# RWKV recurrence with a split-precision channel MLP: Q as one scan over padded decays, batch 0's state sum moved from TensorE to VectorE, and a new order table

## The chip, the cores and the metric

The kernel runs on one core of one Trainium2 chip. The metric is the device time in microseconds of one execution, lower is better. The kernel before was run three times: 462.59, 463.63 and 464.78 us, median 463.63. The profiled execution took 464.79 us.

## The reference

Two parts follow each other. The first is a recurrence over 768 time steps for 4 batches x 8 heads of width 48, the second a token mix of rank 32 and a channel MLP with a hidden layer of 1536.

```python
for t in range(S):                                   # B, H, S, D = 4, 8, 768, 48
    cur = einsum('bhd,bhe->bhde', u * k[t], v[t])
    y[t] = einsum('bhd,bhde->bhe', r[t], state + cur)
    state = w[t][..., None] * state + einsum('bhd,bhe->bhde', k[t], v[t])
x = y with heads side by side                         # (4, 768, 384)
xt = x.transpose(0, 2, 1)
u = x + (xt @ U @ V).transpose(0, 2, 1)               # U: 768 x 32, V: 32 x 768
out = u + maximum(u @ w_ch1, 0) @ w_ch2               # 384 -> 1536 -> 384
```

## The kernel before, in words

**Chunks.** The 768 steps of a batch are cut in 6 chunks of 128, so there are 24 chunks, numbered 0 to 23 (batch 0 has 0 to 5). In a chunk the heads lie in NP = 4 pairs j, two heads on the 128 partitions, time along the columns. Decays w are turned into two running products by scans on VectorE: F, from the end of the chunk backwards (`scan_f`, L393, four scans of 128, one for each pair), and Q, the reciprocal of the whole product times the products from the start (`first_q`, L402, a reciprocal of four columns, then `scan_q`, L407, four scans of 127). The scans add the tile `zeros`, a broadcast of one column of the PSUM tile `bank`, which also holds dS, the state increment of a chunk. The steps of a chunk, by the names that the table of the order uses: LW, LRK, LV, LKR load; F, T (totals), R and Q as told; RP and KS scale r by Q and k by F; MD or RK, RU, RED make the diagonal, SEL and SEL2 put it in A; AM (L519) makes the scores in PSUM, CP (L522) copies them into A under a mask; KT and KN turn k; DS (L529) makes dS; ZM multiplies the state by the next chunk's total decay; YA and YZ (L589 to L616) make the output, XE copies it out, XT and XN turn it for the token mix.

**State.** In chunks 1 to 4 of batch 0, ZP (L538) first puts the old state into dS by a matmul with the identity, DS adds to it, and ZM reads the sum from PSUM. In the other batches DS stands alone, ZA (L561, VectorE) adds the old state, and ZM reads SBUF.

**Weights and MLP.** Weights come as 64-bit numbers and are decoded and split in a high and a low part, a piece of 128x384 at a time: AB and E on ScalarE, C1 (L271), C2 (L278), SG, ADD (L295), HI, and SUB (L343) for the low part. w1 has pieces 0 to 11 (named w10 to w111), w2 has pieces w20 to w211. Each half batch then runs 12 up-projections UP b.half.f (L805) and 3 x 4 parts of the down-projection DN b.half.ct.part (L840), each nine matmuls of 384 columns; HH and HL (L818) split a hidden block in high and low. DN 0.0.2.0 needs w28, DN 0.0.2.1 needs w29, and so on. GSL is the last step of a batch's token mix.

**Order.** Nothing is scheduled by the compiler here. `ORDER` (L52 to L93) is a string with three characters for each of the 1438 steps: two for the step's number, one for its engine and for how many filler matmuls `warm` issues on TensorE ahead of it. `plan` turns it into a list; each engine runs its steps in that list's order, and a step that has to wait holds up all that stands behind it on its engine. `caps` gives the buffers of each kind: one for the scores, three for MLP results in PSUM, two for w.

```python
zeros = zero.broadcast_to([P, P])
copy(eng, st["tot"], st["F"][:, :, 0])
ENG[eng].tensor_tensor(out=rk[:, 0], in0=rk[:, 0], in1=st["Q"], op=ALU.mult)
```

Of the kernel before, what the change touches and what calls it, by code (L numbers as in the profile page):

```python
# [38 lines left out]
def channel_order():  # L39
# [18 lines left out]
    "5K00518u04+08d06004-05L01M05p05M18f15w00k15-01v00612909L05i01L08Z09200U06605q00J08g18v06F05j05r05m01N01O11u0"
    "0W08c05y14Y08a06704Z06808b15Q05R06G08h00V08x08y15n08W01P16909K05o16H00X01w01Q00Y05s00Z11x00F05t01y18m08z08+0"
    "0a06I01R18i08j19316A01z06B00G06J09008n06C02R02B06D00b06N06E09N00m01B06K06L01D08q0Ao08w01E01+09406M08k09501C0"  # L60
    "1F18-09U01-09O18l01G19P00o0Af06O06P06S06T06X06W16Q09802A02C09606U09n06Y06b06V08o02D06Z09M08p09906a02E19A0970"
    "9S00n09109C09D06f00p02T00q16x09Q06R12F12G09V01H00r19B09a07102H06g09b06h09W10s01T00t19m06y07208r01V06z01U01W0"
    "1k01m01I07306c07701X11l09R16l02S09X01Y10u09p01n02U01Z01a07806m09v01o01p12V09F09G09u09Y09e00w09r09s09Z02W19c0"
    "0v06d12j07906n0A006e09H01q06u00x01r00y00z19d06r02X06v02l06+06w02I01s02k02-06s12Y10+12006t06-19E10-0A102K02Z0"
    "7409t17006i02m02J02n01017509I02o17602109o07S03102p02a02q02r06o02202L02302402s02519f06j06p07T02M03Z02N1380A20"
    "AC09h02b0260271280DA09i06q07U06k02d0A402O07W07a07X02t02c02u02v02e02w02P02x02f12Q13H02y03002g02h07Y03A07b09w0"
    "2z03203Q03302i13903402+13B07A07B03503I03K03603C03D1AE03J03707c03L07C07D07G07H07V13E0AD03S03F03R09q19j09x17d0"
    "9y13M13T03G13U03a07E07Z07I07J03N17M07K07k0AF07F03O17L07h03c07l03d03P19T0Ae03b09J03e1AK13f17m07N09z03V0AS03W0"
    "9+0AM07i07j03g07e0AN08907f17g03h13X0AG0AL08A08B0AO17t09g17z07u03Y0A507v0AT09-1A307O0Ap0Aq07+07-0800An07n0AH0"
    "8107o0AI0D-0AJ08207P0A70AP0A80A61AQ1Db07Q0AU08Y1ES0AW09k07q0Ah0Aj0Ak0AR0AV0Al07R0Am07p07r1830Ar0A90DZ0Dj0Di0"  # L70
    "Dk07s09l07w0DJ0Au0As0AZ0Aa0Ag0Ab08408s0Da0DK0850DL18t0Dc08C07x07y08608D0870880DM0Ac0E90At08E08F0De0Df0DN1Ad0"
    "Av0AX0Ai0AY0D90DC0Aw0Dd0DE0Ax0E00AA0AB08I08J0DH1EA0EB08K0Dg1DF0DG1Ay0DB0EC0DO1Dl08L0Dm0Az0A-0A+08M0B00Dh0E20"
    "B10DR0E80E70E40E50B20DP0Dn0Do18O0B30Et0FT0DS08P0B40B50B60B70DI0B808Q0E308G0DQ1B90DD08R0FU0Ew0Dp0BA0ER0BD0BE0"
    "DT0BB1BF0FV0DV0BG1Ea0Dr08S08H08N0BC0E61Ds0C70BH0Eu0BW0DU1C80BK0Ey0Eb0Ez0BX1ED0E+1BL0BY0BT0EE0Dq1BM0BI1BJ0BQ0"
# [71 lines left out]
def rwkv_moe_kernel(ctx, tc, wT, rkT, vN, rkN, uB, uT, uD, U, V, w1, w2, out):  # L146
# [35 lines left out]
    zeros = zero.broadcast_to([P, P])  # L182
# [168 lines left out]
    def chunk(g):  # L351
# [8 lines left out]
        def load_w():  # L360
            st["w"] = sb2.tile([P, NP, P], F32, tag="w", name=f"w_{g}", bufs=W_BUFS)
            nc.sync.dma_start(st["w"].rearrange("p j t -> p (j t)"), wT[b, c])

        def load_w2():
            st["w2"] = sb2.tile([P, NP, P], F32, tag="w", name=f"w2_{g}", bufs=W_BUFS)
            nc.sync.dma_start(st["w2"].rearrange("p j t -> p (j t)"), wT[b, c])
# [23 lines left out]
        def scan_f():  # L390
            F = st["F"] = sb2.tile([P, NP, P], F32, tag="F", name=f"F_{g}")
            for j in range(NP):
                nc.vector.tensor_tensor_scan(  # L393
                    out=F[:, j, ::-1], data0=st["w"][:, j, ::-1], data1=zeros, initial=1.0, op0=ALU.mult, op1=ALU.add
                )
# [669 lines left out]
```

## Time and profile before

| what | value |
|---|---|
| median of three runs | 463.63 us (462.59 to 464.78) |
| the profiled execution | 464.79 us |
| its span | 463.1 us, 9864 instructions |
| mean granted TensorE clock | 0.989 of full |
| busy: TensorE, VectorE, ScalarE, GpSimd | 442.9, 308.4, 165.2, 122.7 us |
| first matmul of the MLP (L805) | 68.02 us from the start |
| last matmul (L840) begins | 458.21 us from the start |

The span runs from the first to the last instruction, the run's time has 1.7 us more around it. PE is TensorE, DVE is VectorE, ACT is ScalarE, POOL is GpSimd. Busy time of PE counts a matmul from its issue to its modelled end, and matmuls overlap in the pipeline, so a PE that is 96% busy does not show by itself how much it could still take; the gaps between its instructions and what ended them tell more. Waits name the instruction that came last before an engine went on. The chain of waits is followed back from the last instruction.

### The profile page before, as it was taken

How to read it: one execution, taken by the hardware profiler on the slowest of the kernel's cores; microseconds unless marked ns; L12 is line 12 of the kernel's file. 1: busy time of each engine (PE TensorE's matmuls, PEld its weight loads, DVE VectorE, ACT ScalarE, POOL GpSimd, SP SyncE). 2: the span in 40 equal slices, each digit the busy share in tenths (PEclk: the TensorE clock that was granted, in tenths of full speed). 3: DMA queues.
4: the chain of work that ended last, by engine and by line, in shares of the span. 5: the costliest groups of instructions: out<-in, count | busy, mean ns of one | idle time of the engine just before them, and what ended most of it. 6: DMA issues, size and time to landing. Idle time of an engine off the chain costs nothing.

```text
span 463.1 us, 9864 instructions
## 1 busy us (share of the span) xinstructions
PE 442.9 (96%) x4046; PEld 406.6 (88%) x4049; DVE 308.4 (67%) x653; ACT 165.2 (36%) x406; POOL 122.7 (27%) x127
## 2 busy tenths in 40 slices
PE   8988979899998999999999999999999999999996
PEld 4766558889997989999999989999999899999995
DVE  8898999999865969847685847877166152434410
ACT  4786888796732322123103230411023101300300
POOL 4667667414513346213123220110020010000000
PEclk9799999999998999999999999999999999999999
DMA  7876844374234425114221642201120000110001
GB/s 272 324 253 207 280 146 131 102 272 144 70 93 139 127 84 155 64 48 140 74 89 38 200 141 71 69 33 47 52 64 24 18 17 18 45 42 0 35 18 38
DMA packets 21361, 48.46 MB, mean 105 GB/s; under 512 B 2496, under 2 KB 9024, under 8 KB 21312
## 3 DMA queue, kind: packets, MB, share of 16 engines
q1 hardware_dynamic: 21312, 47.79, 31.3%
q8 instruction: 33, 0.54, 0.5%
q14 instruction: 16, 0.13, 0.1%
HBM read 43.06 MB, written 4.72 MB: 103 GB/s over the span
## 4 chain that ended last, share of the span: by engine, by line
PE 75%; DVE 18%; ACT 3%; issue 2%; DMA 1%; DVEq 0%; ACTq 0%; SPq 0%
PE f L840 29%; PE f L805 28%; PE aps L519 4%; DVE Q L407 3%; PE y L589 2%; DVE F L393 2%; PE bank L529 2%; PE y L599 2%; DVE A L522 1%; DVE hl L818 1%; PE y L612 1%; DVE cva_w L271 1%; DVE cva_w L278 1%; PE trx L649 1%; PE trk L507 1%
## 5 line engine op out<-in xcount | busy, mean ns | idle before, releaser
L805 PE MATMUL f<-u,w1h 128*128 128x384 f32 x576 | 149.9, 341 | 5.6 <-DVE hl L818 5.6
L805 PEld LDWEIGHTS f<-u,w1h 128*128 128x128 f32 x576 | 103.7, 189 | 8.0 <-DVE hl L818 7.3
L840 PE MATMUL f<-hh,w2h 128*128 128x384 f32 x288 | 99.4, 345 | 0.0
L840 PE MATMUL f<-hl,w2h 128*128 128x384 f32 x288 | 97.8, 339 | 0.0
L840 PE MATMUL f<-hh,w2l 128*128 128x384 f32 x288 | 97.3, 338 | 0.4 <-DVE w2l L343 0.4
L805 PE MATMUL f<-u,w1l 128*128 128x384 f32 x288 | 97.5, 338 | 0.0
L818 DVE SCALAR_TENSOR_TENSOR hl<-f,hh 128x384 fp32r<-128x384 f32 x96 | 52.3, 552 | 34.9 <-ACT hh L812 34.0
L812 ACT ACTIVATE hh<-f 128x384 fp32r<-128x384 f32 x55 | 27.0, 496 | 118.1 <-PE f L805 118.1
L840 PEld LDWEIGHTS f<-hh,w2l 128*128 128x128 f32 x288 | 54.0, 188 | 0.7 <-DVE w2l L343 0.7
L805 PEld LDWEIGHTS f<-u,w1l 128*128 128x128 f32 x288 | 54.4, 189 | 0.0
L840 PEld LDWEIGHTS f<-hl,w2h 128*128 128x128 f32 x288 | 54.2, 188 | 0.1
L840 PEld LDWEIGHTS f<-hh,w2h 128*128 128x128 f32 x288 | 54.0, 187 | 0.2 <-issue 0.2
L459 POOL TENSOR_SCALAR_AFFINE_SELECT A<-dv 128x512 f32<-128x512 f32 x32 | 21.5, 679 | 85.0 <-PE y L599 45.9
L393 DVE TENSOR_TENSOR_SCAN F<-w,bank 128x128 f32<-128x128 f32 x96 | 32.3, 398 | 11.2 <-DMA w<-in_wT 6.5
L407 DVE TENSOR_TENSOR_SCAN Q<-w,Q,bank 128x127 f32<-128x127 f32 x96 | 38.0, 458 | 2.6 <-ACT Z L570 1.2
L814 DVE TENSOR_SCALAR hh<-f 128x384 fp32r<-128x384 f32 x41 | 22.4, 550 | 24.6 <-PE f L805 24.6
L855 DVE TENSOR_TENSOR xT<-f,xT 128x384 f32<-128x384 f32 x24 | 13.2, 551 | 35.9 <-PE f L840 35.9
L522 DVE COPY_PREDICATED A<-maskf,aps 128x1024 f32<-128x1024 uint32 x24 | 31.3, 1304 | 5.7 <-PE aps L519 5.7
L519 PEld LDWEIGHTS aps<-rk 48*128 48x128 f32 x384 | 24.5, 195 | 6.1 <-issue 3.0
L519 PE MATMUL aps<-rk 48*128 48x128 f32 x384 | 29.1, 293 | 0.6 <-POOL rk L414 0.6
L414 POOL TENSOR_TENSOR rk<-rk,Q 128x512 f32<-128x512 f32 x14 | 21.8, 1558 | 27.1 <-DVE Q L407 21.5
L764 POOL TENSOR_TENSOR u<-xT,u 128x384 fp32r<-128x384 f32 x9 | 10.5, 1173 | 62.9 <-ACT u L758 62.2
(125 smaller groups left out, 592.9 us busy)
## 6 DMA issues: line engine op xcount, KB each, us to landing
rk<-in_rkT SPq DMA_DIRECT2D x24, 512.0 KB, 4.2
raw_w<-in_w SPq DMA_DIRECT2D x24, 384.0 KB, 5.1
w<-in_wT SPq DMA_DIRECT2D x30, 256.0 KB, 2.8
kr<-in_rkN SPq DMA_DIRECT2D x18, 384.0 KB, 3.4
v<-in_vN SPq DMA_DIRECT2D x24, 224.0 KB, 3.4
out_dram<-xT SPq DMA_DIRECT2D x24, 192.0 KB, 1.9
raw_V<-in_V SPq DMA_DIRECT2D x1, 192.0 KB, 4.1
raw_U<-in_U SPq DMA_DIRECT2D x1, 192.0 KB, 5.7
```

What stands on the lines that cost most here:

```text
L393: nc.vector.tensor_tensor_scan(out=F[:, j, ::-1], data0=st["w"][:, j, ::-1], data1=zeros, initial=1.0, op0=ALU.mult, op1=ALU.add)
L407: nc.vector.tensor_tensor_scan(out=Q[:, j, 1:P], data0=st["w"][:, j, 0 : P - 1], data1=zeros[:, 1:P], initial=Q[:, j, 0:1], op0=ALU.mult, ...
L414: ENG[eng].tensor_tensor(out=rk[:, 0], in0=rk[:, 0], in1=st["Q"], op=ALU.mult)
L459: nc.gpsimd.affine_select(out=A[:, i], in_=dv[:, NP * i : NP * i + NP].unsqueeze(2).broadcast_to([P, NP, P]), pattern=[[0, NP], [1, P]], c ...
L519: nc.tensor.matmul(aps[:, i, j, :], rk[r, 1, j, :], rk[r, 0, j, :], start=True, stop=True)
L522: nc.vector.copy_predicated(flat(st["A"]), mask8, flat(st["aps"]))
L805: nc.tensor.matmul(ps, wt[:, f, ct, :], u[ct][:, z], start=(n == 0), stop=(n == 8))
L812: nc.scalar.activation(hh, d["ps", f], AF.Relu)
L814: nc.vector.tensor_scalar(out=hh, in0=d["ps", f], scalar1=0.0, scalar2=None, op0=ALU.max)
L818: nc.vector.scalar_tensor_tensor(out=hl, in0=d["ps", f], scalar=0.0, in1=hh.bitcast(F32), op0=ALU.max, op1=ALU.subtract)
L840: nc.tensor.matmul(d["o", ct], wt[:, 4 * ct + part, f - 3 * part, :], hid[f][z], start=(part == 0 and n == 0), stop=(part == 3 and n == 8),)
L855: nc.vector.tensor_tensor(out=o, in0=d["o", ct], in1=o, op=ALU.add)
```

## The change

The decays are stored in segments of SEG = 129 columns, of which column 0 is padding with the value 1. `first_q` writes the four reciprocals into this padding of the w tile, and `scan_q` is one scan of 4 x 129 = 516 columns from the initial value 1: at the end of a segment the running product is back at 1, and the next padding multiplies by that pair's reciprocal. The Q tile has the same segments; RP reads their first 128 columns. F, the check of w (`check_w`) and the loads are changed to the new layout, a load of w being 129/128 of what it was. Q's tile is taken by step Q, no longer by step R, and R now uses w. In batch 0, ZP and the accumulation on top of it are gone: DS writes dS alone, and ZA and ZM work as in the other batches, with four ZA more on VectorE.

```diff
+SEG = P + 1
-    zeros = zero.broadcast_to([P, P])
+    zeros = zero.broadcast_to([P, NP * SEG])
...
-            st["w"] = sb2.tile([P, NP, P], F32, tag="w", name=f"w_{g}", bufs=W_BUFS)
+            st["w"] = sb2.tile([P, NP, SEG], F32, tag="w", name=f"w_{g}", bufs=W_BUFS)
...
         def first_q():
-            st["Q"] = sb2.tile([P, NP, P], F32, tag="Q", name=f"Q_{g}")
-            nc.vector.reciprocal(st["Q"][:, :, 0], st["F"][:, :, 0])
+            nc.vector.reciprocal(st["w"][:, :, 0], st["F"][:, :, 0])
 
         def scan_q():
-            Q = st["Q"]
-            for j in range(NP):
-                nc.vector.tensor_tensor_scan(
-                    out=Q[:, j, 1:P], data0=st["w"][:, j, 0 : P - 1], data1=zeros[:, 1:P], initial=Q[:, j, 0:1],
-                    op0=ALU.mult, op1=ALU.add,
-                )
+            st["Q"] = sb2.tile([P, NP, SEG], F32, tag="Q", name=f"Q_{g}")
+            flat = lambda t: t.rearrange("p j s -> p (j s)")
+            nc.vector.tensor_tensor_scan(
+                out=flat(st["Q"]), data0=flat(st["w"]), data1=zeros, initial=1.0, op0=ALU.mult, op1=ALU.add
+            )
...
-                        dS[r, j, i * D : i * D + D], kn[:, j, r], v[:, j, r], start=not carry,
-                        stop=not carry or j == NP - 1,
+                        dS[r, j, i * D : i * D + D], kn[:, j, r], v[:, j, r], start=True, stop=True,
...
-            if carry:
-                zp = step("ZP " + nm, "PE", state_old, [old["z"]], take=[buf["dS"]], use=[old["buf"]["Z"]])
-                ds = step("DS " + nm, "PE", state_add, [kn, lv, zp], use=[buf["dS"], buf["kn"], buf["v"]])
-            else:
-                ds = step("DS " + nm, "PE", state_add, [kn, lv], take=[buf["dS"]], use=[buf["kn"], buf["v"]])
-            from_ps = c == 0 or carry
+            ds = step("DS " + nm, "PE", state_add, [kn, lv], take=[buf["dS"]], use=[buf["kn"], buf["v"]])
+            from_ps = c == 0
...
 ORDER = (
-    "3i03j03k03n03p03q03v03s14800703w+4B04903m03o13x03r13y00804a04b03+60900A04D01b01105104000B03-03z14J14G04E04K2"
+    "3i03j03n03v03p03k04803q03o03r03w+4B04903x04D04E03s04003+04a03-04d00703m04b01b01105104A03y03z14100900804J04G0"
...
```

All 40 lines of the table are new. 197 steps that are in both kernels change their engine: HH mostly swaps between ScalarE and VectorE (22 one way, 18 the other), and XN (8 of them), KN, T, XE, XU, RP, KS, SEL, SUB, ADD and others move. In sum VectorE has 11 steps fewer, ScalarE 8 more, GpSimd 7 more, and TensorE the four ZP fewer. The fillers on TensorE go from 49 half units to 64: MD 1 has 7 more ahead of it, DS 0 has 5, AM 1 has 7, DS 2 has 6, and KT 0, VM V1, MD 2 and AM 4 lose 10 together. No copy in the diff gets a choice of engine that it did not have; the three PSUM copies of the change's short description can only be such reassignments by the table.

**The first place: VectorE in chunks 3 to 6.** In a name such as F_5_606 the 5 is the chunk and 606 the buffer's own number; `bank_94` holds dS and the zeros. Before:

```order
L522 COPY_PREDICATED A_3_444<-maskf_102,aps_3_557 128x1024
L393 SCALAR_TENSOR_TENSOR F_5_606<-w_5_545,bank_94 128x128 x4
L402 RECIPROCAL Q_5_611<-F_5_606 128x4
L393 SCALAR_TENSOR_TENSOR F_6_616<-w_6_550,bank_94 128x128 x4
L407 SCALAR_TENSOR_TENSOR Q_5_611<-w_5_545,Q_5_611,bank_94 128x127 x4
L522 COPY_PREDICATED A_4_664<-maskf_102,aps_4_593 128x1024
```

and after the change:

```order
L407 SCALAR_TENSOR_TENSOR Q_4_528<-w_4_295,bank_94 128x516
L394 SCALAR_TENSOR_TENSOR F_5_549<-w_5_423,bank_94 128x128 x4
L272 TENSOR_SCALAR cva_w1_2_547<-cva_w1_2_547 128x384
L549 TENSOR_TENSOR Z_2_570<-bank_94,Z_1_466 128x384
L402 RECIPROCAL w_5_423<-F_5_549 128x4
L325 TENSOR_TENSOR Vst_118<-vm_0_443,Vst_118 32x384
L521 COPY_PREDICATED A_3_531<-maskf_102,aps_3_579 128x1024
```

The four Q scans are one row of 516 columns, the reciprocal goes to w, and a ZA (L549) that reads `bank` stands between the scans.

**The second place: VectorE in chunks 9 to 11**, at the end of batch 0's MLP. Before:

```order
L522 COPY_PREDICATED A_9_1717<-maskf_102,aps_9_1433 128x1024
L818 SCALAR_TENSOR_TENSOR hl_0_1_7_1810<-f1_0_1_7_1774,hh_0_1_7_1809 128x384
L402 RECIPROCAL Q_10_1834<-F_10_1665 128x4
L407 SCALAR_TENSOR_TENSOR Q_10_1834<-w_10_1442,Q_10_1834,bank_94 128x127 x4
L414 TENSOR_TENSOR rk_10_1606<-rk_10_1606,Q_10_1834 128x512
L818 SCALAR_TENSOR_TENSOR hl_0_1_8_1837<-f1_0_1_8_1813,hh_0_1_8_1836 128x384
L447 TENSOR_REDUCE dv_10_1876<-kr_10_1719 128x8
L855 TENSOR_TENSOR xT_0_0_337<-f2_0_0_2_1644,xT_0_0_337 128x384
L393 SCALAR_TENSOR_TENSOR F_11_1936<-w_11_1690,bank_94 128x128 x4
```

and after the change:

```order
L806 SCALAR_TENSOR_TENSOR hl_0_1_7_1815<-f1_0_1_7_1804,hh_0_1_7_1814 128x384
L413 TENSOR_TENSOR rk_10_1319<-rk_10_1319,Q_10_1774 128x512
L394 SCALAR_TENSOR_TENSOR F_11_1836<-w_11_1772,bank_94 128x128 x4
L402 RECIPROCAL w_11_1772<-F_11_1836 128x4
L521 COPY_PREDICATED A_9_1690<-maskf_102,aps_9_1426 128x1024
L802 TENSOR_SCALAR hh_0_1_5_1874<-f1_0_1_5_1856 128x384
```

The copy of the scores CP 9 (A_9) stood eight rows ahead of F 11; now F 11 stands ahead of CP 9.

## Rows read from the trace of the kernel before

**Rows 1.** Page, part 1: busy us, share of the span, instructions.
```profile
PE 442.9 (96%) x4046; PEld 406.6 (88%) x4049; DVE 308.4 (67%) x653; ACT 165.2 (36%) x406; POOL 122.7 (27%) x127
```

**Rows 2.** Busy time in four stretches (us from the start), PE clock, DMA, GB/s.
```profile
0.00:68.00 68.00, 58.55 (x779) 40.67 (x782) 61.02 (x143) 49.23 (x129) 43.18 (x47) 0.95 0.73 245
68.00:114.00 46.00, 42.46 (x380) 39.66 (x376) 45.11 (x88) 37.71 (x77) 22.52 (x21) 1.00 0.50 168
114.00:160.00 46.00, 43.36 (x412) 40.55 (x411) 33.98 (x73) 18.88 (x52) 14.06 (x15) 0.96 0.33 104
160.00:459.00 299.00, 298.55 (x2484) 285.68 (x2482) 168.11 (x351) 59.39 (x152) 42.95 (x46) 1.00 0.20 64
```

**Rows 3.** Waits of PE: total us, times, longest.
```profile
PE f L805 <- DVE hl L818: 5.6, 5, 1.9
...
PE f L840 <- DVE w2l L343: 0.4, 1, 0.4
```

**Rows 4.** Waits of DVE from 0 to 135 us: total, times, longest.
```profile
...
DVE Q L407 <- ACT Z L570: 1.2, 1, 1.2
...
DVE Q L407 <- PE bank L529: 0.8, 1, 0.8
DVE F L393 <- PE bank L529: 0.7, 1, 0.7
DVE F L393 <- PE bank L538: 0.6, 1, 0.6
```

**Rows 5.** DVE groups, 0 to 114 us: count | busy us, mean ns | idle before.
```profile
L407 DVE TENSOR_TENSOR_SCAN Q<-w,Q,bank 128x127 f32<-128x127 f32 x40 | 15.8, 457 | 2.3 <-ACT Z L570 1.2 <-PE bank L529 0.8
L393 DVE TENSOR_TENSOR_SCAN F<-w,bank 128x128 f32<-128x128 f32 x40 | 13.4, 397 | 2.5 <-DMA w<-in_wT 0.9 <-PE bank L529 0.7 <-PE bank L538 0.6
...
L343 DVE TENSOR_TENSOR w1l<-cva_w,w1h 128x384 fp32r<-128x384 f32 x4 | 4.5, 1118 | 0.0
...
L561 DVE TENSOR_TENSOR Z<-bank,Z 128x384 f32<-128x384 f32 x2 | 1.1, 555 | 0.2 <-PE bank L529 0.2
```

**Rows 6.** DVE in order of time from 5 us: start, us, instruction.
```profile
...
5.38 1.59 DVE L407 TENSOR_TENSOR_SCAN Q<-w,Q,bank 128x127 f32<-128x127 f32 x4
6.89 0.66 DVE L418 TENSOR_TENSOR rk<-rk,F 128x508 f32<-128x508 f32 x1
7.47 1.35 DVE L393 TENSOR_TENSOR_SCAN F<-w,bank 128x128 f32<-128x128 f32 x4
8.73 0.66 DVE L271 TENSOR_SCALAR cva_V<-cva_V 128x192 f32<-128x192 f32 x1
```

**Rows 7.** All engines in order of time, from 71 us.
```profile
...
75.22 0.35 DVE L271 TENSOR_SCALAR cva_w<-cva_w 128x384 f32<-128x384 f32 x1
...
78.41 2.13 DVE L271 TENSOR_SCALAR cva_w<-cva_w 128x384 f32<-128x384 f32 x2
...
79.11 1.21 POOL L418 TENSOR_TENSOR rk<-rk,F 128x508 f32<-128x508 f32 x1
```

**Rows 8.** Chain of waits, 136 to 145.5 us: start, us, what.
```profile
...
136.31 0.52 PE bank L529 x16
...
136.85 1.36 DVE F L393 x4
...
142.33 3.00 PE f L805 x9
```

**Rows 9.** Two stretches, columns as in Rows 2.
```profile
12.80:20.00 7.20, 7.20 (x73) 5.73 (x75) 7.02 (x15) 5.05 (x18) 5.08 (x5) 0.53 0.85 311
142.00:146.00 4.00, 3.67 (x15) 3.24 (x17) 1.66 (x4) 1.19 (x3) 1.59 (x2) 0.58 0.64 214
```

**Rows 10.** Chain of waits, around 115 us.
```profile
...
115.00 3.15 PE f L805 x18
118.14 1.59 PE f L840 x9
```

**Rows 11.** Chain of waits, around 22 us.
```profile
...
21.74 0.75 PE bank L538 x2
```

More of the change, by code (lines that the diff above doesn't have):

```diff
@@ L58 @@
[L58 to L62, printed above, removed]
@@ L360, in load_w @@
         def load_w():
[L361 to L362 removed]
+            st["w"] = sb2.tile([P, NP, SEG], F32, tag="w", name=f"w_{g}", bufs=W_BUFS)
+            nc.sync.dma_start(st["w"].rearrange("p j s -> p (j s)"), wT[b, c])
         def load_w2():
[L365 to L366 removed]
+            st["w2"] = sb2.tile([P, NP, SEG], F32, tag="w", name=f"w2_{g}", bufs=W_BUFS)
+            nc.sync.dma_start(st["w2"].rearrange("p j s -> p (j s)"), wT[b, c])
         def load_rk():
@@ L393, in scan_f @@
                 nc.vector.tensor_tensor_scan(
-                    out=F[:, j, ::-1], data0=st["w"][:, j, ::-1], data1=zeros, initial=1.0, op0=ALU.mult, op1=ALU.add
+                    out=F[:, j, ::-1], data0=st["w"][:, j, SEG - 1 : 0 : -1], data1=zeros[:, 0:P], initial=1.0, op0=ALU.mult, op1=ALU.add
                 )
@@ L421, in check_w @@
             nc.scalar.activation(
-                junk, st[which].bitcast(U32), AF.Relu, bias=b_max, scale=2.0**-23, accum_out=guard[:, g : g + 1]
+                junk, st[which][:, :, 1:SEG].bitcast(U32), AF.Relu, bias=b_max, scale=2.0**-23, accum_out=guard[:, g : g + 1]
             )
@@ L426, in chunk @@
         st["tots"] = step("T " + nm, "DVE", totals, [f], use=[buf["F"]], alt="ACT")
-        rc = step("R " + nm, "DVE", first_q, [f], take=[buf["Q"]], use=[buf["F"]])
-        q = step("Q " + nm, "DVE", scan_q, [rc], use=[buf["w"], buf["Q"]])
+        rc = step("R " + nm, "DVE", first_q, [f], use=[buf["F"], buf["w"]])
+        q = step("Q " + nm, "DVE", scan_q, [rc], take=[buf["Q"]], use=[buf["w"]])
         rp = step("RP " + nm, "DVE", scale_r, [q, lr], use=[buf["Q"], buf["rk"]], alt="Pool")
@@ L529, in state_add @@
                     nc.tensor.matmul(
-                        dS[r, j, i * D : i * D + D], kn[:, j, r], v[:, j, r], start=not carry,
-                        stop=not carry or j == NP - 1,
-                    )
-        carry = b == 0 and c > 0
-        def state_old():
-            flat_z = lambda t: t.rearrange("p j n -> p (j n)")
-            nc.tensor.matmul(flat_z(dS), ident, flat_z(old["Z"]), start=True, stop=False)
+                        dS[r, j, i * D : i * D + D], kn[:, j, r], v[:, j, r], start=True, stop=True,
+                    )
         on = c < NCH - 1
@@ L887, in recurrence @@
                 st, vt = (full(xtp, "xT", f"{n}_{j}") for n in ("st", "vt"))
-                nc.sync.dma_start(chunks(wt), wb[:, :, j * P : (j + 1) * P])
+                nc.sync.dma_start(chunks(wt), wb[:, :, j * SEG + 1 : (j + 1) * SEG])
                 nc.sync.dma_start(chunks(rt), rb[:, 0, j])
@@ L1020, in chunked @@
         return t
-    wT = chunked(w, 1.0).reshape(B, NCH, P, NP * P)
+    wT = np.ones((B, NCH, P, NP, SEG), f32)
+    wT[..., 1:] = chunked(w, 1.0)
+    wT = wT.reshape(B, NCH, P, NP * SEG)
     rkT = np.stack([chunked(r, 0.0), chunked(k, 0.0)], axis=3)
```

75 lines of the change are left out of this document (40 added, 35 removed).

## The prediction

> **What bounds the kernel now.** The page's busy shares come first [rows 1]: TensorE 96%, VectorE 67%. They are averages over stages with different limits, so the second view is busy time by stretch [rows 2]. Read its VectorE column (the third): 61.0 of the first 68 us, 45.1 of the next 46, then 34.0 of 46, then 168 of 299. Read its TensorE column (the first): 9.5 us idle in the first 68 us, 3.5 in the next 46, 2.6 up to 160 us, and 0.45, the last drain, in the 299 us after that. So the run has two halves. Up to about 114 us VectorE is full and TensorE takes what it is fed; from 160 us on TensorE is full. The end moves with the moment at which TensorE has caught up with its feeders, and with little else. VectorE work that is saved after 160 us is worth nothing: TensorE covers it, and that cover is 299 us long.
>
> The third view, the waits of TensorE [rows 3], says which feeder ends last: HL on VectorE, 5.6 us in five waits, and once the low part of a w2 piece, 0.4 us. VectorE's own waits [rows 4] are few: four of them, 3.3 us together, are scans that read the zeros in `bank` and stand behind something that reads or writes dS in the same tile.
>
> **The scans.** Four Q scans take 1.51 us (5.38 to 6.89), four F scans 1.26 us (7.47 to 8.73) [rows 6]. Forty of each lie before 114 us [rows 5], so ten chunks. One scan of 516 columns is not in the trace. Upper bound: four F scans, 4 x 128 = 512 columns with four starts, 1.27 us. Lower bound: the F rows without three of their four starts. A scan is recorded with 397 ns and follows the next after 315, so some 80 ns are pipeline; three starts of that size leave 1.02 us. I take 1.15, the middle, so 0.36 us saved for a chunk (0.24 to 0.49), 3.6 us over ten chunks. The reciprocal is as long as before; 1% more to load is hidden by loads that run a chunk ahead.
>
> **The gate.** What counts is VectorE's work ahead of a step that TensorE needs, plus TensorE's work left behind it. I counted steps in both orders up to DN 0.0.2.1, the down-projection part that needs w29 on VectorE; DN steps around here are where TensorE waited for a w2 piece. VectorE: ten Q scans give back 3.6. Four ZA in batch 0 cost 4 x 0.5 = 2.0 (0.55 recorded, some 0.5 back to back [rows 5]). The table moves eight more steps of other kinds ahead of it (two SUB, two ADD, two HI and others) at some 0.5 us, 4.0, and one F fewer, 1.3. The SUB rows go up to 1.1 us [rows 5], so this could be 1 more. Sum: -3.6 + 2.0 + 4.0 - 1.3 = +1.1 us. TensorE: one UP more is done by then, 3.15 / 2 = 1.6 us [rows 10], and one DS fewer, 0.5 us [rows 8], so 1.1 us less is left. **The gate therefore moves by 0.0** (-1.3 to +2.2 from the two prices above): the scans' time is spent on work that the new order pulls ahead. That is the main reason why I expect little.
>
> At intermediate steps VectorE comes earlier: up to GSL 0 the steps of other kinds fall by 3.6 us and four ZA add 2.0, and eight Q scans give 2.9, so some 4.5 us. The MLP would start at about 63.5 us instead of 68. It is given back by the gate above.
>
> **ZP.** Its four matmul pairs (0.75 us each [rows 11], 3.0 in sum) leave TensorE in the first 68 us, where it idles for 9.5 [rows 2]; the new fillers stand there too. I cost both at nothing; VectorE is the cover. [...] Fillers that kept the clock up there would find VectorE in the way.
>
> **Early waits of VectorE.** Two of the four have lost their cause: ScalarE no longer reads `bank` to make Z in chunks 1 to 4 (1.2 us), and there is no ZP to write it (0.6) [rows 4]. In exchange four ZA on VectorE must wait for DS on TensorE, and F, R and Q queue behind them. One such wait of 0.6 us is my guess from the size of the rows that stay (0.7, 0.8). Net **-1.2 us**, bounds -3.3 (all four go) and +1.4 (each ZA waits 0.8, less the 1.8).
>
> **The stop at 140 us.** F 11 began 0.02 us after the matmul on `bank` ended [rows 8], behind it stood Q, CP and HL, and TensorE then waited 1.9 us for HL [rows 3]. From 142 to 146 us the clock was 0.58 [rows 9], which cost 4 x 0.42 = 1.7 us more: 3.6 in all. In the new order F 11 stands ahead of CP 9, and the scores AM 10 need the one score buffer that CP 9 frees; DS 10 comes after AM 10, so F 11 cannot wait for DS 10. That stop is gone as such. But the same stretch now has CP 9 behind F 11, so something else may be late; I take 40% of it, **-1.4 us**, bounds -3.6 and the rival below.
>
> **GpSimd.** Five two-input steps fewer run on GpSimd ahead of the gate, eleven steps more after it. The same C1 takes 0.35 us alone and over 1 us with a GpSimd step in the same microseconds [rows 7]. [...] I keep the plain sum, since no row tells which instructions would meet.
>
> **Sum.** 464.8 for the profiled execution, 0.0 - 1.2 - 1.4 = -2.6, so 462.2. The median of the runs lies 1.2 under the profiled execution, so **461.0 us** for the median. A measurement of this kernel can tell some 0.5%, 2.3 us, from no change; the forecast lies just beyond that.
>
> **The rivals.**
>
> *A new stop in chunks 9 to 11 (slower, 0.22).* From SUB w29 to CP 9 VectorE has 14.8 us of work in the new order by the same step prices; TensorE from DN 0.0.2.1 to AM 10 has 8 UP, 3 DN, a DS and a transposition, 18.2 us. So 3.4 us of VectorE waits in that stretch are free; beyond that TensorE stops at AM 10, the clock falls as it did at 142 us, and each 2 us stop costs 3.6 to 3.7. Two stops in place of one are +3.7, with the early gain of 1.2: 463.6 + 2.5 = 466.1 us, more if the ZA also wait. For it: the lead of VectorE's work over TensorE's is here 7 us against 6 before, and CP 9 stands behind a load-dependent F 11. Against it: VectorE is only 74% busy in that stretch now [rows 2].
>
> *Nothing moves (same, 0.16).* The early waits are replaced by waits for DS, and one stop like the old one remains: 463.6 us, or up to 1.2 less. For it: the gate's sum is zero.
>
> *More than the sum (faster, 0.22).* The early start holds: VectorE's prices ahead of the gate fall, three early waits go (-2.5) and the stop goes whole (-3.6): 463.6 - 6.1 = 457.5 us. For it: up to w28, one step earlier than the gate, the VectorE sum is 2 us lower than before.
>
> **How the numbers follow.** The forecast has 0.40, within 459.5 to 462.5, of which 0.25 lie under 461.3 (faster by over 0.5%) and 0.15 above. Faster: 0.25 + 0.22 = 0.47. Same: 0.15 + 0.16 = 0.31. Slower: 0.22. The range is 456.5 to 467: it takes in the three rivals with the upper bound of the gate, and leaves a tenth on either side.
>
> **What would show it.** Right: a first L805 matmul at about 63 to 65 us, L407 with 24 instructions of about 1.15 us, no L538, scans waiting less on `bank`, TensorE's wait on w2l or HL near 110 us as before, no clock drop near 142 us, TensorE without gaps after 160 us. Wrong: Q scans at 1.27 us or more; ZA waiting for DS by over 1 us each; a TensorE stop with a clock row near 0.5 between 110 and 150 us; TensorE gaps after 160 us, which no part of the sum has.

## The result, and the profile after

The changed kernel takes 447.14 us (median of 4 runs, 445.99 to 448.49), beside it the kernel before 463.79 (462.59 to 464.78): ratio 0.964, 95% interval 0.961 to 0.968. The forecast was 461.0 in a range of 456.5 to 467.0. The sign was right, the size was not: 16.6 us in place of 2.6. The profiled execution took 445.99 us, its span is 444.3, 18.8 less than before. (It is the fastest of its four runs, and the profiled execution of the kernel before is the slowest of its four, so the traces lie 2.2 us further apart than the medians.)

Busy time, the page's first part (against [rows 1]), then the stretches of [rows 2]; the last one ends earlier because the kernel does:

```profile
PE 434.9 (98%) x4048; PEld 400.8 (90%) x4048; DVE 281.9 (63%) x570; ACT 168.3 (38%) x420; POOL 125.9 (28%) x134
```
```profile
0.00:68.00 68.00, 63.86 (x824) 47.20 (x825) 65.19 (x145) 55.61 (x138) 45.36 (x52) 1.00 0.75 252
68.00:114.00 46.00, 45.30 (x398) 42.94 (x397) 42.71 (x89) 35.80 (x81) 18.34 (x18) 1.00 0.46 152
114.00:160.00 46.00, 46.00 (x509) 41.84 (x509) 36.43 (x71) 16.81 (x47) 17.46 (x19) 1.00 0.49 156
160.00:440.00 280.00, 279.76 (x2331) 268.83 (x2325) 137.24 (x267) 60.03 (x155) 44.75 (x48) 1.00 0.19 61
```

TensorE's idle time is 4.1 us in the first stretch (9.5 before), 0.7 in the second (3.5), none in the third (2.6, and the clock was 0.96 there). VectorE is 26.5 us less busy over the whole span, though it has four sums more: the scans, 0.35 us less in each of 24 chunks, are 8.4 of that. All of TensorE's waits of 0.3 us or more, against [rows 3], and those of VectorE up to 135 us that count, against [rows 4] (total, times, longest):

```profile
PE y L577 <- DVE A L521: 1.6, 2, 1.0
PE idle L188 <- DVE bank L182: 1.3, 1, 1.3
PE bank L528 <- ACT raw_w L268: 0.9, 1, 0.9
PE gb L689 <- ACT xn L160: 0.3, 1, 0.3
PE aps L518 <- DVE rk L417: 0.3, 1, 0.3
...
DVE hh L802 <- PE f L793: 3.0, 4, 1.4
DVE hl L806 <- ACT hh L800: 1.3, 2, 0.7
```

The waits for HL are gone, and so are the four waits of scans on `bank`. In the MLP VectorE now waits for TensorE, not TensorE for VectorE; the longest wait for VectorE that is left behind the setup (`idle`) is for the masked copy CP (L521), 1.0 us. VectorE's groups from 0 to 114 us, against [rows 5] (count | busy us, mean ns | idle before):

```profile
L394 DVE TENSOR_TENSOR_SCAN F<-w,bank 128x128 f32<-128x128 f32 x44 | 14.7, 396 | 0.8 <-DMA w<-in_wT 0.8
L407 DVE TENSOR_TENSOR_SCAN Q<-w,bank 128x516 f32<-128x516 f32 x10 | 12.2, 1218 | 0.1
...
L549 DVE TENSOR_TENSOR Z<-bank,Z 128x384 f32<-128x384 f32 x6 | 3.3, 549 | 0.0
L344 DVE TENSOR_TENSOR w1l<-cva_w,w1h 128x384 fp32r<-128x384 f32 x5 | 2.7, 556 | 0.0
```

The last row is the one that the forecast passed by. The same instruction took 1118 ns in the mean before, 556 now. Where the MLP begins, in order of time (start, us):

```profile
57.81 0.60 PE L793 MATMUL f<-u,w1h 128*128 128x384 f32 x2
```

Before, its first row was at 68.02. Call this moment the start and what follows it, span less start, the rest. The start is 10.2 us earlier, the rest 8.6 us shorter (395.0 to 386.5).

### The profile page after: what moved, and what is told of

The parts are those of the page before. It is cut to its first block, busy times and chain, and to the rows that moved or that the text cites. A ratio compares the mean times of both kernels' runs of the same rounds, so it can differ in the third digit from the quotient of the medians.

```text
span 444.3 us, 9807 instructions
## 1 busy us (share of the span) xinstructions
PE 434.9 (98%) x4048; PEld 400.8 (90%) x4048; DVE 281.9 (63%) x570; ACT 168.3 (38%) x420; POOL 125.9 (28%) x134
## 4 chain that ended last, share of the span: by engine, by line
PE 85%; DVE 10%; ACT 3%; DMA 1%; issue 1%; DVEq 0%
PE f L828 34%; PE f L793 30%; PE aps L518 4%; PE idle L188 2%; PE y L577 2%; PE bank L528 2%; PE trx L637 2%; PE y L587 2%; PE trk L506 2%; PE y L600 1%; DMA w<-in_wT 1%; DVE cva_w L279 1%; DVE hl L806 1%; DVE cva_w L272 1%; PE hp L734 1%; DVE Q L407 1%
## 5 line engine op out<-in xcount | busy, mean ns | idle before, releaser
L793 PE MATMUL f<-u,w1h 128*128 128x384 f32 x576 | 148.4, 339 | 0.0
L800 ACT ACTIVATE hh<-f 128x384 fp32r<-128x384 f32 x59 | 28.3, 491 | 113.9 <-PE f L793 113.9
L752 POOL TENSOR_TENSOR u<-xT,u 128x384 fp32r<-128x384 f32 x16 | 16.6, 1043 | 120.8 <-ACT u L746 88.9
L802 DVE TENSOR_SCALAR hh<-f 128x384 fp32r<-128x384 f32 x37 | 20.5, 555 | 30.1 <-PE f L793 29.9
L521 DVE COPY_PREDICATED A<-maskf,aps 128x1024 f32<-128x1024 uint32 x24 | 31.6, 1317 | 9.8 <-PE aps L518 8.5
L417 POOL TENSOR_TENSOR rk<-rk,F 128x508 f32<-128x508 f32 x18 | 20.1, 1115 | 37.1 <-DMA rk<-in_rkT 16.3
L407 DVE TENSOR_TENSOR_SCAN Q<-w,bank 128x516 f32<-128x516 f32 x24 | 29.3, 1220 | 0.2
L518 PE MATMUL aps<-rk 48*128 48x128 f32 x384 | 27.9, 284 | 0.3 <-DVE rk L417 0.3
L456 ACT ACTIVATE A<-ident,dv 128x128 f32<-128x128 f32 x72 | 22.9, 392 | 13.5 <-DVE dv L446 7.2
```

Source lines behind the costliest of these rows:

```text
L407: nc.vector.tensor_tensor_scan(out=flat(st["Q"]), data0=flat(st["w"]), data1=zeros, initial=1.0, op0=ALU.mult, op1=ALU.add)
L417: ENG[eng].tensor_tensor(out=k, in0=k, in1=st["F"][:, :, 1:P], op=ALU.mult)
L456: nc.scalar.activation(A[:, i, j], ident, AF.Copy, scale=dv[:, NP * i + j : NP * i + j + 1])
L518: nc.tensor.matmul(aps[:, i, j, :], rk[r, 1, j, :], rk[r, 0, j, :], start=True, stop=True)
L521: nc.vector.copy_predicated(flat(st["A"]), mask8, flat(st["aps"]))
L793: nc.tensor.matmul(ps, wt[:, f, ct, :], u[ct][:, z], start=(n == 0), stop=(n == 8))
```

## The experiments

The theories at the start: **M, meetings:** a VectorE instruction that meets a GpSimd one is stretched (w1's SUB on VectorE up to 114 us: 1118 ns in the mean before, 556 after), and the new table has fewer meetings. **P, parts:** the scan and the missing matmuls shorten the chains. **S, sequence:** the order of the steps itself brings the gain. **C, the clock:** the fillers keep TensorE's clock up (from 12.8 to 20 us 0.53 before [rows 9], 1.00 after).

The table has every run; what each one changes is told in the parts that follow. Start, rest and stretched come from one trace of each kernel. *Stretched* is VectorE's time ahead of the end of w29's low part: for each instruction, its duration less the median of the same step without a GpSimd instruction beside it, summed where that is over 0.05 us, with the count. The ratios are to the kernel before, run on the same chip.

| kernel | median us | ratio (95%) | start | rest | stretched |
|---|---|---|---|---|---|
| before | 463.8 | 1 | 68.0 | 395.0 | 14.5 (25) |
| after | 447.1 | 0.964 (0.961 to 0.968) | 57.8 | 386.5 | 7.3 (13) |
| order_alone | 447.5 | 0.964 (0.956 to 0.972) | 59.7 | 386.9 | 5.2 (9) |
| parts_old_order | 464.9 | 1.002 (0.998 to 1.005) | 73.0 | 390.9 | 16.0 (26) |
| a_4scan | 447.4 | 0.966 (0.957 to 0.974) | 58.4 | 386.8 | 7.2 (12) |
| a_zp | 448.5 | 0.966 (0.958 to 0.975) | 59.7 | 386.5 | 5.5 (9) |
| b_short | 454.8 | 0.982 (0.978 to 0.986) | 63.3 | 389.6 | 2.1 (7) |
| a_short | 442.8 | 0.958 (0.955 to 0.961) | 56.0 | 384.9 | 1.3 (5) |
| b_newtable | 452.6 | 0.977 (0.974 to 0.981) | 63.1 | 389.8 | 8.0 (15) |
| a_nofill | 449.8 | 0.973 (0.970 to 0.976) | 61.6 | 386.5 | 7.3 (12) |
| b_1scan | 459.7 | 0.989 (0.985 to 0.993) | 65.1 | 390.8 | 15.9 (27) |
| b_fill | 463.6 | 0.997 (0.994 to 1.000) | 67.0 | 395.8 | 14.4 (24) |
| b_fill_1scan | 459.6 | 0.988 (0.984 to 0.993) | 67.0 | 390.9 | 15.4 (27) |
| b_short_1scan | 448.8 | 0.969 (0.961 to 0.976) | 61.1 | 386.0 | 1.4 (4) |
| a_short_nofill | 447.2 | 0.965 (0.957 to 0.973) | 60.5 | 384.9 | 1.3 (4) |
| t_p1 | 478.1 | 1.034 (1.023 to 1.045) | 68.3 | 405.4 | 25.1 (39) |
| t_p3 | 476.6 | 1.027 (1.019 to 1.035) | 67.3 | 407.8 | 17.2 (33) |
| q1 | 450.5 | 0.972 (0.967 to 0.977) | 61.3 | 388.0 | 11.0 (20) |
| q2 | 449.9 | 0.972 (0.966 to 0.978) | 60.1 | 388.0 | 9.8 (19) |
| q3 | 447.1 | 0.966 (0.960 to 0.971) | 63.0 | 386.3 | 8.3 (16) |

### The table apart from the parts

The first four: new table with old parts, old table with new parts, and one part undone at a time. Four scans in the padded layout, for order_alone and a_4scan:

```diff
-            flat = lambda t: t.rearrange("p j s -> p (j s)")
-            nc.vector.tensor_tensor_scan(
-                out=flat(st["Q"]), data0=flat(st["w"]), data1=zeros, initial=1.0, op0=ALU.mult, op1=ALU.add
-            )
+            for j in range(NP):
+                nc.vector.tensor_tensor_scan(
+                    out=st["Q"][:, j, :], data0=st["w"][:, j, :], data1=zeros[:, 0:SEG], initial=1.0, ...
```

In order_alone and a_zp, ZP is as before the change and ZA 1 to 4 are out of the table; in parts_old_order, ZP is out and ZA k stands behind DS k.

> The new table with the old parts: four Q scans a chunk, and the old state put into dS by a matmul with the identity instead of the sum on VectorE. Theory M (meetings): before w29 VectorE lost 14.5 us in the kernel before, and 7.3 us after, in instructions that stretched while a GpSimd instruction ran beside them; the table sets who meets whom, so the table brings most of the 16.6 us: 451 us (448 to 454), stretched VectorE time ahead of w29 under 10 us, first MLP matmul at 59 to 62 us. Rival P (parts): the single scan and the missing matmuls bring most through shorter chains from engine to engine: 458 to 463 us, first MLP matmul at 65 us or later.

> The old table with the new parts: one Q scan a chunk, and batch 0's state added on VectorE directly behind DS, where the matmul's place was. Theory M: the scans save 3.5 us ahead of w29 and the sums cost 0.9 more there than they did (two more of 0.5 us), meetings stay near 14 us: 460 us (457 to 463). Rival P: 447 to 453 us.

> The changed kernel with four Q scans of 129 columns a chunk instead of one of 516; all else as changed. The scans are 0.36 us a chunk longer, ten chunks lie ahead of w29: if VectorE's work sets the end there, 3.6 us slower, 450.7 us (449.5 to 452). If the scans lie beside other work (TensorE sets the end), 447 us (within 1). If four starts break the new table's timing, over 453 us.

> The changed kernel with the old state put into dS by TensorE again for chunks 1 to 4 (DS 2 goes a few steps later, behind the step that frees dS); all else as changed. VectorE has four sums of 0.5 us less, TensorE 3 us more in the first 60 us. If VectorE's work sets the end: 445 us (444 to 447). If the matmuls' waits on the scans' zeros in the same PSUM tile and the longer chain to Z matter: 449 us (447.5 to 452), with scans of VectorE waiting on bank again, 2 us in sum.

The table with old parts takes 447.5, with the stretched time (5.2 us) and the start (59.7) that theory M gave, and is 3.5 us faster than its 451, just under its range. The parts in the old table give nothing (464.9, over both forecasts): the scan's gain is there, but the four sums wait for TensorE (total, times, longest, up to the start):

```profile
DVE Z L549 <- PE bank L528: 8.0, 4, 2.8
```

So ZA needs the table that fits it. Undoing either part in the new table costs less than the runs can tell (0.3 and 1.4 us). a_zp came out inside the second of its forecasts, with one Q scan that waits 2.2 us; the trace puts that wait down to a step of ScalarE, not to `bank`. a_4scan missed its first forecast for a reason of its own: its scans are shorter than those of before (all 96, count | busy us, mean ns; b_newtable has the old form):

```profile
L407 DVE TENSOR_TENSOR_SCAN Q<-w,bank 128x129 f32<-128x129 f32 x96 | 32.5, 400 | 0.2
```
```profile
L407 DVE TENSOR_TENSOR_SCAN Q<-w,Q,bank 128x127 f32<-128x127 f32 x96 | 37.9, 456 | 2.6 <-ACT cva_w L254 2.2
```

From start to next start that is 1.29 us a chunk against 1.51, and 1.16 for one scan. Most of the 0.35 comes with the constant start value in place of one read from `Q`; three starts are only 0.13. At 0.13 us a chunk a_4scan cannot tell its own two theories apart. So order_alone was not the table alone, and a run for that follows.

### Meetings taken away, the old code with the new table, fillers

In b_short and a_short GpSimd's two-input steps shrink to 16 columns; what they would have made of the other columns is left out, and where a low part is missing TensorE reads the high part in its place:

```diff
+    def few(eng, t, on=True):
+        if eng != "Pool" or not on:
+            return t
+        return t[:, 0:16] if len(t.shape) == 2 else t[:, 0:1, 0:16]
-            ENG[eng].tensor_tensor(out=rk[:, 0], in0=rk[:, 0], in1=st["Q"], op=ALU.mult)
+            ENG[eng].tensor_tensor(out=few(eng, rk[:, 0]), in0=few(eng, rk[:, 0]), in1=few(eng, st["Q"]), op=ALU.mult)
...
```

b_newtable is the old code with only `ORDER` replaced, by the table of order_alone; a_nofill sets the filler counts of MD 1 (8), DS 0 (5), AM 1 (7), XT 0.0 (7) and DS 2 (6) to 0.

> The kernel before, with its two-input GpSimd steps cut to 16 columns (0.1 us in place of about 1 us; where a low part is then missing TensorE reads the high part instead, so its work is the same). Same table, same steps, same waits, so only the time that GpSimd runs is gone, and with it the meetings on VectorE. Theory M: the 14.5 us of stretched VectorE time ahead of w29 falls under 4, and most of it comes back at the end, since VectorE sets the end up to 114 us: 453 us (449 to 457). Rival S (the sequence itself, not the meetings, makes the new table faster): 460 to 464 us. TensorE waited for GpSimd only 0.6 us in this kernel, so shorter GpSimd steps by themselves are worth at most about 1 us.

> The same cut of GpSimd's steps in the changed kernel. 3.7 us of stretched VectorE time lie ahead of the first MLP matmul there, 7.3 us ahead of w29, and TensorE has no gaps behind the first MLP matmul but 0.7 us. Theory M: the MLP starts up to 3 us earlier, the end is 444.5 us (443 to 446.5), and the two tables differ by less than 10 us once the meetings are gone (16.6 with them). Rival S: they still differ by 14 us or more.

> The code before without any edit but the new table (the matmuls with the identity stand directly ahead of their DS, batch 0's sums left out of the table). Against the run with the padded layout and four scans (447.5 us) only the Q scan's form is different: it starts from an element in memory and takes 1.51 us a chunk in place of 1.29. If VectorE's work up to the first MLP matmul sets the end: 8 x 0.22 = 1.8 us more, 449.3 us (448 to 450.5). If it has slack: 447.5 us.

> The changed kernel without its fillers, but for the 31 at the first step: 33 half-units fewer, 7 us of TensorE work. If VectorE is what bounds the first 58 us, fillers cost and give nothing: 447 us (446 to 448), though the clock falls to half around 12 to 20 us. [...]

**Meetings are shown.** With 2.1 us of stretched time in place of 14.5 the old kernel takes 454.8, inside what M gave (449 to 457); a_short takes 442.8, just under its range. In the kernel before, one of them looks like this, VectorE and GpSimd in order of time (start, us):

```profile
73.65 1.65 DVE L343 TENSOR_TENSOR w1l<-cva_w,w1h 128x384 fp32r<-128x384 f32 x1
...
73.27 1.61 POOL L414 TENSOR_TENSOR rk<-rk,Q 128x512 f32<-128x512 f32 x1
```

GpSimd's ends at 74.88, VectorE's 0.42 us later: 1.23 of its 1.65 us lie ahead of GpSimd's end, and the 0.42 behind it are less than the 0.55 us that it takes alone. The group of this line up to 140 us (ns min/median/max), before and then with the GpSimd steps cut:

```profile
L343 DVE TENSOR_TENSOR w1l<-cva_w,w1h x4: 550/1138/1648, 43.3 to 93.3; 128x384 fp32r<-128x384 f32 x4
```
```profile
L354 DVE TENSOR_TENSOR w1l<-cva_w,w1h x4: 530/552/959, 40.6 to 85.2; 128x384 fp32r<-128x384 f32 x4
```

But the rest of the theory did not hold: the two tables still differ by 12.0 us without meetings, between M's bound of 10 and S's 14. b_newtable says where some of it is: 452.6, 3 to 4 us over the forecast and 5 to 6 over order_alone, for 1.8 us of scans ahead of the start. The scans' price moved the meetings too (8.0 against 5.2), and TensorE ran short at 50 to 60 us, where order_alone has it busy for 9.83 us at clock 1.00 (PEclk is the third number from the end):

```profile
50.00:60.00 10.00, 8.26 (x76) 4.55 (x64) 9.90 (x24) 7.95 (x19) 4.83 (x5) 0.87 0.77 261
```

a_nofill goes theory C's way: 449.8 us, over the 446 to 448 of its forecast and 2.7 us slower than the changed kernel, the start 3.8 us later, though VectorE's work ahead of it is the same. Two stretches after the change, then the same without fillers:

```profile
10.00:20.00 10.00, 9.96 (x157) 7.25 (x156) 9.91 (x22) 9.27 (x28) 6.73 (x8) 1.00 0.99 352
20.00:30.00 10.00, 9.99 (x171) 7.76 (x169) 9.77 (x23) 9.76 (x29) 9.17 (x10) 1.00 0.98 339
```
```profile
10.00:20.00 10.00, 7.67 (x85) 6.46 (x83) 8.30 (x16) 7.40 (x25) 5.82 (x6) 0.70 0.97 336
20.00:30.00 10.00, 9.89 (x148) 7.48 (x146) 7.75 (x19) 8.03 (x22) 6.07 (x7) 0.79 0.78 266
```

The third busy column is VectorE: 19.7 of 20 us with fillers, 16.1 without. The granted clock without fillers is 0.70 and 0.79, with them 1.00 in both stretches. VectorE's own long waits without fillers are for ScalarE (total, times, longest, up to the start), and the changed kernel has neither:

```profile
DVE A L521 <- ACT A L456: 1.7, 1, 1.7
DVE cva_V L296 <- ACT raw_V L287: 1.6, 1, 1.6
```

ScalarE in turn waits 11.7 us for TensorE from 8 to 32 us, against 7.9 with fillers.

### Scan and fillers in the old table

b_1scan is the changed code with ZP and the old `ORDER`; b_fill is the kernel before with 8, 5, 7 and 6 half-units at MD 1, DS 0, AM 1 and DS 2.

> The kernel before with the padded layout and one Q scan a chunk, old table and matmuls kept. 8 chunks of 0.36 us lie ahead of the first MLP matmul, 10 ahead of w29. If VectorE's work sets the end as the prediction's sum has it: 2.9 to 3.6 us faster, 460.5 us (459.5 to 461.5). If the meetings fall differently, as where the table did not fit the new prices: 458 to 465 us, with a stretched time ahead of w29 that differs from 14.5 us by what is missing.

> The kernel before with 25 more half-units of filler ahead of four early steps (8 ahead of MD 1 in place of 1, 5 ahead of DS 0, 7 ahead of AM 1, 6 ahead of DS 2, as the new table has them). Without its fillers the changed kernel began the MLP 3.8 us later, all of it idle time of VectorE behind a TensorE at half clock. Theory C (the clock in the first 30 us): the granted clock is 1.00 from 10 to 20 us, the MLP starts at 64 to 65.5 us, 460 us (458.5 to 461.5). Rival, the prediction's own words (fillers would find VectorE in the way): 463.6 us, within 1.

> Both: old table, padded layout with one Q scan, 25 more half-units of filler. If the two add up: 2.9 and 3.8 us ahead of the first MLP matmul, which then comes at 61 us, 457 us (455 to 459). Under 453 us the sequence of the steps would have no part in the gain; over 459 us the old sequence holds the gain back.

The scan alone gives 4.1 us by the medians and 5.0 by the ratio, over the 2.9 to 3.6 of the sum. The fillers give nothing, though they do what they should: the row of [rows 9] becomes

```profile
12.80:20.00 7.20, 6.86 (x96) 4.95 (x94) 7.16 (x16) 6.64 (x20) 5.02 (x6) 1.00 0.89 313
```

Clock 1.00 in place of 0.53, and VectorE busy 7.16 us in place of 7.02. In the old table it was full there anyway, as the prediction said; in the new one it is not. Scan and fillers together, 459.6, give no more than the scan alone.

### Is it the sequence?

> The old table and its matmuls with one Q scan a chunk, and GpSimd's two-input steps cut to 16 columns: no meetings, and the scans' price of after. If the scan (4.1 us alone in the old table) and the meetings (8 us alone) add up: 450.5 us (449 to 452). It leaves some 8 us to the changed kernel with the same cut (442.8), which only the sequence of the steps, the fillers and ZA can be.

> The changed kernel with GpSimd's steps cut and without its 33 half-units of filler. If the fillers are worth 2.7 us here as they are with the meetings: 445.5 us (444.5 to 446.5). Against the old table with one scan and the cut, what is then left between the two is the sequence of the steps and ZA alone. If VectorE, without meetings, has the slack to bear a half clock: 443 us.

For the most part no. The old sequence without meetings and with one scan takes 448.8, the new one without meetings and its fillers 447.2; the first is 0.2 us under its range, the second 0.7 over. By the ratios they differ by 1.7 us. That, within what these runs can tell, is what sequence and ZA have together, less what the old table's own fillers are worth: 18 half-units, 7 of them at XT 0.0 as in the new table, still stand in the first of the two, and no run takes them away alone. In ratios times 463.8 the way from before to after is: GpSimd's steps cut -8.3, one scan -6.2, new table with ZA but no early fillers -1.7, fillers -3.4, GpSimd's steps back +3.1. So of 16.6 us the scan has about 6, fewer meetings about 5 (8.3 less 3.1), the fillers about 3; each is good to some 2 us (by the medians the fillers are 4.4 without meetings and 2.7 with them), and they don't add up in every order (with the old table's meetings the scan gives 4 and the fillers nothing). The cut of GpSimd's steps also shortens what waits for them, so 8.3 is an upper bound on meetings; TensorE waited 0.6 us for GpSimd in the kernel before.

### Other tables

t_p1 and t_p3 are the changed code with two more tables, found by counting with the durations of the traces, meetings counted too. Steps up to 150 us move, 92 and 75 change their engine.

> The changed kernel with another table: up to about 150 us the steps other than loads are moved to other places in their queues, and 92 of them go to their other engine, so that by the durations of the traces fewer VectorE instructions meet GpSimd ones and the last VectorE step ahead of the first MLP matmul comes some 3.5 us earlier. The loads keep their order, the fillers their steps. In the changed kernel the end lies 386.6 us behind that step. Theory (TensorE is saturated from the MLP's start on, and only this start counts): MLP at 54 to 55.5 us, 442.5 us (441 to 444.5). If something behind the start breaks (a wait on a piece of w2, the clock): 445 to 450.

> A second such table, found apart from the first, 75 steps on their other engine: the same theory gives 443 us (441 to 445); the two tables differ in which steps stand where, so that both being faster would speak for the rule (start of the MLP plus 386.6 us) and not for one lucky place.

Both are the worst kernels of the study, 30 us behind the changed kernel, with 39 and 33 meetings. The count had forecast 442 to 443. Their start is 10 us later than after the change, the rest 19 to 21 us longer. Two stretches of t_p1 (TensorE idle for 9.9 and 10.0 us, clock 0.90 and 0.96):

```profile
0.00:68.00 68.00, 58.15 (x745) 39.77 (x745) 62.74 (x117) 43.77 (x113) 45.38 (x51) 0.90 0.69 234
68.00:114.00 46.00, 36.01 (x337) 31.71 (x337) 39.36 (x73) 29.12 (x60) 20.08 (x21) 0.96 0.45 150
```

In t_p3 TensorE waits for HL again (total, times, longest; 4.3 us in t_p1):

```profile
PE f L793 <- DVE hl L806: 11.1, 6, 3.5
```

Meetings alone do not explain this: t_p3 has 17.2 us of stretched time and b_1scan, 17 us faster, has 15.9. What broke in these two tables was not taken apart.

Then single moves were made in the changed kernel's own table. q1: CP 5 behind AM 5, C1 w111 behind ZM 4, XN 0.5 ahead of HI w111, GS 0 and GSL 0 ahead of SG w11 and F 8, HP 0.0.0 ahead of DS 6, KS 7, ULP 0.0.1, ULP 0.0.2 and SUB w11 ahead of weight steps, SG w16 and ADD w16 behind UHP 0.0.2. q2: also F 1 ahead of RP 0. q3: F 1 and the two first moves of q1, and C1 w19 behind CP 1.

> The changed kernel with a few steps of its table set one to ten places elsewhere, all between 41 and 58 us, read from its trace: CP 5 ahead of C1 w111 (TensorE waited 1.0 us for CP 5, and C1 w111 met a GpSimd step, 0.8 us), XN 0.5 and GS 0 ahead of weight steps on ScalarE, GSL 0 ahead of F 8 (it was ready 1.3 us before its turn), the last two low parts of the MLP's input ahead of weight steps. The chain to the first MLP matmul is shorter by about 1.0 + 0.4 + 0.8 us, at most 3. Rule (the end lies 386.6 us behind the last VectorE step ahead of the first MLP matmul): 445 us (443.8 to 446.5). If the pieces of w1 that these steps delay become late, or new meetings take the gain: 446.5 to 450 us.

> The same, and F 1 ahead of RP 0 on VectorE (RP 0 met KS 0 on GpSimd, 0.8 us). If early work of VectorE counts one to one: 0.5 to 0.8 us under q1. As everything behind it shifts, the meetings fall anew: 443 to 448 us.

> The changed kernel with four steps of its table moved: F 1 ahead of RP 0 (which met KS 0, 0.8 us), C1 w19 behind CP 1 (in q1 and q2 the ScalarE step ahead of C1 w19 ended 0.07 us later or more, so that C1 w19 began 0.1 us behind RP 2 on GpSimd in place of 0.1 us ahead of it, and three steps lost 2.0 us; behind CP 1 that race is gone), CP 5 ahead of C1 w111 (TensorE waited 1.0 us for it, and C1 w111 met a GpSimd step). The late edits of q1 are left out. If the meetings of 15 to 21 us are what made q1 slower than the changed kernel: 446 us (445 to 447.5). If it was the edits behind 41 us, CP 5 among them: 448 to 450 us.

q1 is 3.4 us slower and q2 2.7, both over their forecasts. The moves of q1 start at 41 us, yet at 17 us it is 1.0 us behind already. The changed kernel at 15 us, VectorE, GpSimd, ScalarE:

```profile
15.61 0.36 DVE L272 TENSOR_SCALAR cva_w<-cva_w 128x384 f32<-128x384 f32 x1
...
15.71 1.31 POOL L413 TENSOR_TENSOR rk<-rk,Q 128x512 f32<-128x512 f32 x1 [0.21 <-DVE Q L407]
...
15.02 1.07 ACT L255 ACTIVATE cva_w<-raw_w 128x384 f32<-128x384 f32 x2
```

And q1:

```profile
15.69 1.29 DVE L272 TENSOR_SCALAR cva_w<-cva_w 128x384 f32<-128x384 f32 x1 [0.19 <-ACT cva_w L255]
...
15.58 1.19 POOL L413 TENSOR_TENSOR rk<-rk,Q 128x512 f32<-128x512 f32 x1 [0.21 <-DVE Q L407]
```

The step w19 on VectorE began 0.10 us ahead of RP 2 there and 0.11 us behind it here, and took 0.36 or 1.29 us; two more meetings followed, 2.2 us in all. What set the two times apart before 41 us, where the order of the steps is the same, stays open. With that race taken out, q3 is the changed kernel's equal, not better. Its six runs fall into two groups, four from 446.6 to 447.2 us and two at 451.1 and 451.3; the profiled one, at 451.08, began the MLP at 63.0. No version that keeps GpSimd's whole steps beat the changed kernel.

## Why the prediction was wrong

**The scans: right in size.** The forecast was -3.6 us up to the gate; the ten Q scans ahead of w29 take 15.1 us before and 11.6 after, -3.5. The middle of two bounds hit by luck: the upper one, four F scans at 1.27 us, has the constant start value in it without saying so (four Q scans of that form take 1.29), and the lower one took three starts for 0.25 us, where they are 0.13. For ZA the forecast was +2.0, and +2.1 was measured.

**"Eight more other steps at some 0.5 us, 4.0": the step that failed.** The eight steps are there, but all VectorE work ahead of w29's low part falls from 107.6 to 99.4 us. Of -8.2, -3.5 are Q, +2.1 ZA, -1.2 the F, so the other steps are -5.6 in place of +4.0. The stretched time, 14.5 us before and 7.3 after, explains 7.2 of these 9.6; the other 2.4 stay open. The sum priced the steps that the table adds and let all others keep the time that they had in the old order, meetings included (1118 ns for an instruction of 556), as if a price belonged to an instruction and not to its neighbour on another engine. So the gate did not move by 0.0: w29's low part ends at 104.8 us in place of 117.3, 8.2 us from work and 4.3 from waits.

**"I keep the plain sum": the paragraph on GpSimd.** A row stood there (C1 takes 0.35 us alone, over 1 us with a GpSimd step beside it [rows 7]) and got no price in the sum, because no row told who meets whom. The trace of before tells more: five of VectorE's ten SUB take 0.97 to 1.65 us, against 0.55 alone; each of the five began while a GpSimd instruction ran and ended 0.41 to 0.42 us behind it (more in the last part). Asking in the trace of before which durations lay over their own minimum, 25 instructions and 14.5 us, would have bounded the term; how much of it the new order keeps, 7.3 us, only the run told.

**"Given back by the gate": wrong.** The MLP started at 57.8, not at 63.5, and nothing was given back. In six traces of the new table (after, order_alone, a_zp, a_4scan, a_nofill, q3), with starts from 57.8 to 63.0, the rest is 386.3 to 386.9 us: TensorE is busy for 376 of the 377 us from 63 to 440 in each, so the end moves with the start (where TensorE runs short behind the start, as in b_newtable, q1 and q2, it is 388.0 to 389.8; with GpSimd's steps cut it is 384.9). In the kernel before it was 395.0, and TensorE waited 5.6 us for HL behind the start [rows 3], because VectorE still ran behind; one scan and no meetings together bring 386.0 there too (b_short_1scan).

**The early waits of VectorE:** the forecast was -1.2 us; the time up to the gate in which VectorE does no work falls by 4.3 (9.7 to 5.4), beyond the bound of -3.3. ZA did not wait; in the old table it waited 8.0 (parts_old_order).

**ZP and fillers, costed at nothing with VectorE as the cover.** For the fillers this was true in the old table (b_fill) and false in the new, where that cover was gone: 2.7 us (a_nofill, which takes away the 7 half-units at XT 0.0 too, that both tables have). The condition was written down and then not asked of the new order. No run takes ZP away alone; a_zp, which puts it back in place of ZA, is 1.4 us slower, less than the runs can tell.

**The stop at 140 us** was taken at 40%, 1.4 of 3.6 us; it went whole: TensorE is busy 46.00 of 46 us from 114 to 160 at clock 1.00.

**The rivals.** No new stop came; of the three, "more than the sum" had the right direction and, with 6.1 us, a third of the size.

## To carry to other kernels

Before costing a moved VectorE step, split its row into minimum and excess, and look whether GpSimd runs beside the long ones: here the excess belonged to the order (14.5 us before, 7.3 after). Find the moment from which the last engine is full, and forecast that moment; what came behind it here was a constant (386.3 to 386.9 us in six traces). And a table has to be run to be priced: 0.1 us decided 0.9 us in q1, and two tables that were better by the count lost 30.

## What was not expected of the hardware

Only some forms were stretched. In the traces of before and after, instructions with two SBUF inputs (SUB, RK, RU, RP, UL, ADD, ZM) reach 1.25 to 1.65 us and short forms with one (C1, C2, T) 0.98 to 1.43. Of those that read PSUM none was stretched, though GpSimd ran beside them: 11 ZA took at most 0.56 us, 31 CP at most 1.33, 48 HL at most 0.56, the same as without it. Nor were the scans, which read one SBUF and one PSUM operand: with GpSimd beside them 108 F took at most 0.42 us, 42 Q of 127 columns at most 0.48, 14 Q of 516 at most 1.23, the same as without it.

The stretched ones ended a fixed time behind GpSimd's. In the two traces 50 VectorE instructions are over 0.05 us longer than the median of their form without a neighbour. Every one of them began while a GpSimd instruction ran, and ended behind it: by 0.41 to 0.42 us in the 21 with two inputs of 384 columns, by 0.54 to 0.55 in the 4 with two of 512, by 0.21 to 0.22 in the 22 C1 and C2 of 384, by 0.03 in the 3 T. A GpSimd instruction can be the long one, too, and beside more than one of VectorE's. Before, start and us:

```profile
31.75 3.82 POOL L414 TENSOR_TENSOR rk<-rk,Q 128x512 f32<-128x512 f32 x1 [3.42 <-DVE kr L475]
...
34.34 1.32 DVE L522 COPY_PREDICATED A<-maskf,aps 128x1024 f32<-128x1024 uint32 x1
```

Eight VectorE instructions of such forms stand back to back beside this RP on GpSimd, none of them stretched; it ends at 35.57, 1.23 us after the CP, the first that reads PSUM, begins. The shortest RP on GpSimd in this trace takes 1.28 us.

A scan that starts from an element in memory takes 456 ns for 127 columns, from a constant 400 for 129; one of 516 takes 1218, so a further start costs 0.04 us (0.13 for three, above). A scan is also slower by the column than SUB: 1.16 us for 516 columns against 0.47 for the 384 of SUB, 2.2 against 1.2 ns a column from start to start.
